# Block products for the first feed-forward's down projection, with a new order of the first batch's attention

## The chip, the cores and the metric

One core of a Trainium2 chip runs the kernel. The metric is the device time of one execution in microseconds (us), the median of several. TensorE (PE) multiplies into PSUM, a memory of eight banks; VectorE (DVE), ScalarE (ACT) and GpSimd (POOL) work on tiles in SBUF; SyncE (SP) issues nearly all transfers. A tile of 128x512 fp32 fills one PSUM bank.

## The reference

```python
kv  = einsum('bhsd,bhse->bhde', k, v)          # 4 batches, 8 heads, 576 rows, 64 wide
out = einsum('bhsd,bhde->bhse', q, kv)
x   = out / sqrt(mean(out*out, -1) + 1e-6) * g_norm      # 2304 tokens x 512
x   = (silu(x @ w_gate) * (x @ w_val)) @ w_out           # hidden 1536, weights in float64
y   = softplus(x @ w2_in) @ w2_out                       # hidden 2048, weights in float64
```

## The kernel before

Tokens lie in five tiles: one of 512 columns for each of the four batches (t = 0 to 3), and one of 256 columns for the 64 rows left over in each batch (t = B). Each fp32 product is made of three matmuls: every operand is split into a high part, rounded to fp32r, and a low part, the rest; `mm3` multiplies high by high, low by high and high by low and adds them in one PSUM bank. The high part is a cast on ScalarE, the low part a subtraction on VectorE or GpSimd. Weights come as 64-bit floats and are turned into fp32 by bit operations (`convert`: one ScalarE and three VectorE instructions).

**Attention.** For each batch `kv_step` (four), `q_step` (transposes, four or five), `o_step` and `x_step` run on TensorE. Between `o_step` and `x_step` stands the root: a square on ScalarE, sums and a small scaling on VectorE (L467, L468), a power of -0.5 on GpSimd (L469), and the multiplication with the result on VectorE (L473). Batch 0 is written out by a list of times (`S0`, `NORM0`, `SW`, `Q0`, `S1`); the later batches are woven into the first two hidden blocks of the first feed-forward.

**First feed-forward.** Hidden units go in 12 blocks of 128 (j). For each block and token tile, `ffn1_h` makes gate and value (24 matmuls into one bank each), `silu`, their product u, and u's high and low part (L565, L566). `ffn1_o` multiplies u with four column blocks of `w_out` (12 matmuls, each three into a bank of the pool `po` with three buffers), and VectorE adds each bank to the accumulator `yacc` (L583). The loop goes over j and, in it, over t; the down products of a tile run a tile or two behind its up products (`unit1`, `behind`).

**Second feed-forward.** It goes through pairs of hidden blocks (jp = 0 to 7), first for tokens of t = 0 and 1 (n = 0), then of t = 2 and 3 (n = 1). Its up products are block products already: seven instead of eight (`quad`, tiles hX, hY, hZ). Its down products for n = 1 are seven block products for jp below `LAST2` = 7 (`down2`, tiles dX, dY, dZ, 84 matmuls of 256 columns) and plain ones otherwise (`ffn2_o`, tile pz, 48 matmuls of 512 columns for two tiles). Sums of weight rows that `down2` needs are made beside n = 0 (`row_sums`, tiles pt), written to DRAM and read back.

**Order.** The program's order on every engine is fixed while it is built. A clock of the builder, `now`, runs on with each matmul (`tick`); work of the other engines is put in a queue with a time (`defer`), moved by hand-set shifts by name (`SHIFT`), and written out when the clock passes it. `ENGINE` says for single low parts whether VectorE or GpSimd makes them. On the chip each engine takes its instructions in that order and waits by semaphores.

## Time and profile before

| what | value |
|---|---|
| time, median of 3 runs | 895.47 us (894.54 to 895.49) |
| time of the profiled execution | 895.39 us |
| its span, first to last instruction | 893.3 us |
| TensorE busy | 872.4 us, 98% of the span |
| VectorE, ScalarE, GpSimd busy | 628.5, 352.9, 278.9 us |
| mean granted clock | 0.997 |

The span is 2.1 us shorter than the execution's time. A matmul's end in the profile is modelled, so the pace of matmuls is read from the starts of the next ones, not from their durations.

### The profile page before, as it was taken

The page shows a single profiled execution, that of the slowest core. Times are in us where ns is not written, and L with a number is a line of the kernel's source. Part 1 is how long each engine was busy: PE and PEld are TensorE (multiplying, and loading weights), DVE is VectorE, ACT ScalarE, POOL GpSimd, SP SyncE. Part 2 cuts the span into 40 slices and gives each one's busy share as a digit, 9 for nine tenths or more (in the row PEclk, how much of TensorE's full clock was granted, in tenths as well). Part 3 has the DMA queues.
Part 4 walks back from the last instruction along what each step waited for, and adds up shares of the span by engine and source line. Part 5 has one row for each costly group of instructions (what it writes and reads, how often), then busy time and mean ns, then how long its engine had stood idle before and what let it go on. Part 6 is the DMA issues. An engine that isn't in the chain of part 4 may idle for free.

```text
span 893.3 us, 12775 instructions
## 1 busy us (share of the span) xinstructions
PE 872.4 (98%) x4770; PEld 741.4 (83%) x4770; DVE 628.5 (70%) x987; ACT 352.9 (40%) x614; POOL 278.9 (31%) x211
## 2 busy tenths in 40 slices
PE   5899999999999999999999999999999999999998
PEld 4677788888888888888888888888887889999996
DVE  1865457877878687878687776776887667667564
ACT  3654435333332323233233454444564443444330
POOL 0642302303131312131222373355442132433321
PEclk9999999999999999999999999999999999999999
DMA  9963202234161526160515326667779865444213
GB/s 273 277 178 76 94 1 72 84 129 148 64 195 41 162 86 194 33 209 12 200 41 176 137 95 236 212 237 265 248 247 333 298 209 169 158 141 152 90 48 119
DMA packets 90766, 137.16 MB, mean 154 GB/s; under 512 B 20688, under 2 KB 51664, under 8 KB 90448
## 3 DMA queue, kind: packets, MB, share of 16 engines
q1 hardware_dynamic: 90400, 136.21, 46.4%
q8 instruction: 38, 0.62, 0.3%
q14 instruction: 24, 0.20, 0.1%
q10 hardware_dynamic: 304, 0.13, 0.1%
HBM read 99.09 MB, written 37.22 MB: 153 GB/s over the span
## 4 chain that ended last, share of the span: by engine, by line
PE 89%; DVE 4%; DMA 2%; SPq 2%; ACT 1%; issue 1%; POOL 0%; ACTq 0%; DVEq 0%; POOLq 0%
PE pv L523 16%; PE py L523 16%; PE pg L523 16%; PE pz L523 11%; PE hY L523 8%; PE dY L523 5%; PE hZ L523 4%; PE hr L523 3%; PE dZ L523 2%; PE hX L523 2%; PE pa L453 2%; DMA qr<-in_q_dram 1%; PE dX L523 1%; SPq L276 1%; DMA pt<-pt 1%
## 5 line engine op out<-in xcount | busy, mean ns | idle before, releaser
L583 DVE TENSOR_TENSOR yacc<-yacc,py 128x512 f32<-128x512 f32 (+1 forms) x220 | 136.5, 629 | 50.0 <-PE py L523 49.4
L565 ACT CAST uh<-u 128x512 fp32r<-128x512 f32 (+1 forms) x60 | 34.6, 577 | 168.1 <-DVE u L562 168.1
L523 PE MATMUL hY<-b,wh 128*128 128x512 f32 x384 | 98.2, 391 | 1.6 <-DVE c L908 1.6
L523 PE MATMUL pg<-xh,gh 128*128 128x512 f32 (+1 forms) x240 | 90.0, 375 | 0.0
L523 PE MATMUL pv<-xh,vh 128*128 128x512 f32 (+1 forms) x240 | 89.9, 375 | 0.0
L523 PE MATMUL py<-uh,oh 128*128 128x512 f32 (+1 forms) x240 | 89.5, 373 | 0.2 <-DVE yacc L583 0.2
L523 PE MATMUL py<-uh,ol 128*128 128x512 f32 (+1 forms) x240 | 88.6, 369 | 0.0
L523 PE MATMUL pg<-xl,gh 128*128 128x512 f32 (+1 forms) x240 | 88.5, 369 | 0.1
L523 PE MATMUL pv<-xh,vl 128*128 128x512 f32 (+1 forms) x240 | 88.6, 369 | 0.0
L523 PE MATMUL pg<-xh,gl 128*128 128x512 f32 (+1 forms) x240 | 88.4, 368 | 0.0
L523 PE MATMUL pv<-xl,vh 128*128 128x512 f32 (+1 forms) x240 | 88.4, 368 | 0.0
L523 PE MATMUL py<-ul,oh 128*128 128x512 f32 (+1 forms) x240 | 88.3, 368 | 0.0
L523 PEld LDWEIGHTS hY<-b,wh 128*128 128x128 f32 x384 | 70.2, 188 | 15.3 <-DVE c L908 2.0
L1055 DVE TENSOR_TENSOR zacc<-zacc,pz 128x512 f32<-128x512 f32 x77 | 52.3, 682 | 29.6 <-PE pz L523 29.5
L566 DVE TENSOR_TENSOR ul<-u,uh 128x512 fp32r<-128x512 f32 (+1 forms) x60 | 40.1, 669 | 39.1 <-ACT uh L565 39.1
L872 POOL TENSOR_TENSOR gl<-c,gh 128x512 fp32r<-128x512 f32 x33 | 44.4, 1350 | 53.6 <-ACT gh L870 45.7
L558 ACT ACTIVATE s<-pg 128x512 f32<-128x512 f32 (+1 forms) x60 | 33.2, 554 | 54.4 <-PE pg L523 49.2
L370 POOL TENSOR_TENSOR gl<-gz,gh 128x512 fp32r<-128x512 f32 x12 | 16.3, 1358 | 118.8 <-ACT gh L367 118.8
L523 PEld LDWEIGHTS pg<-xl,gh 128*128 128x128 f32 x240 | 45.2, 188 | 8.2 <-DVE xl L491 0.5
L523 PEld LDWEIGHTS py<-uh,oh 128*128 128x128 f32 x240 | 45.2, 188 | 8.0 <-DVE yacc L583 0.6
L523 PE MATMUL pz<-ph,gl 128*128 128x512 f32 x132 | 51.5, 390 | 0.4 <-POOL gl L872 0.4
L523 PEld LDWEIGHTS py<-ul,oh 128*128 128x128 f32 x240 | 45.1, 188 | 7.8
(198 smaller groups left out, 2059.3 us busy)
## 6 DMA issues: line engine op xcount, KB each, us to landing
wh<-w2d SPq DMA_DIRECT2D x32, 512.0 KB, 6.6
wh<-w2d SPq DMA_DIRECT2D x64, 256.0 KB, 4.7
ir<-in_moe_w_in_dram SPq DMA_DIRECT2D x16, 512.0 KB, 5.8
w2d<-kh SPq DMA_DIRECT2D x32, 256.0 KB, 2.1
w2d<-kl SPq DMA_DIRECT2D x32, 256.0 KB, 2.4
pr<-in_moe_w_out_dram SPq DMA_DIRECT2D x16, 512.0 KB, 6.6
pt<-pt SPq DMA_DIRECT2D x28, 256.0 KB, 6.8
tt<-pt SPq DMA_DIRECT2D x14, 512.0 KB, 6.9
```

The costliest lines, as they stand in the source:

```text
L276: nc.sync.dma_start(t.rearrange("p h c d -> p h (c d)"), src[b, h0:h0 + 4, 0:T, :].rearrange("h (p c) d -> p h (c d)", p=P))
L370: (nc.gpsimd if WLO1 == "g" else nc.vector).tensor_sub(lf, z, f32(hf))
L453: nc.tensor.matmul(pv[p0:p0 + n, hp, :], lhsT=qt[:, hp, p0:p0 + n], rhs=kvm[bb][:, hp, :], start=True, stop=True,)
L523: nc.tensor.matmul(dst, lhsT=a, rhs=b_, start=first and i == 0, stop=last and i == n - 1, skip_group_check=not check)
L558: nc.scalar.activation(s[0], pg, AF.Silu)
L565: nc.scalar.copy(uh, u)
L566: (nc.gpsimd if UL1 == "g" else nc.vector).tensor_sub(ul, u, f32(uh))
L583: defer(ADD1, lambda: nc.vector.tensor_add(a[:, d, :], a[:, d, :], p))
L872: (nc.vector if 0 <= n < len(GLO) and GLO[n] == "v" else nc.gpsimd).tensor_sub(lo, l, f32(hi))
L1055: defer(ADD2, lambda: nc.vector.tensor_add(av[:, m, :], av[:, m, :], p))
```

## The change

The down products of the first feed-forward go by pairs of hidden blocks (2jp, 2jp+1). For two token tiles, four blocks of u and four of `w_out` are multiplied as seven block products instead of eight: `release` makes four differences of u's blocks in place and seven high and low parts; `prep_o` makes four sums of `w_out`'s blocks, and four high and low parts where there were two; `down1` runs the seven products, each two steps of three matmuls, on two banks in turn, and adds the bank after every product to the accumulator before the next product adds to the same bank. Pair 0 (j = 0, 1) and the last pair (j = 10, 11) stay plain, and so does t = B; plain products now add both hidden blocks in PSUM before one addition to `yacc`. The up products are made pair by pair, with `prep_gv` loading and converting their weights. `LAST2` goes from 7 to 6, so that one more pair of n = 1 in the second feed-forward is multiplied plainly. In batch 0 the root is a `Sqrt` on ScalarE and a reciprocal on VectorE, with a table set loaded for it at the start and the one for `silu` after the batch's last `x_step`. `occupy` issues 29 matmuls of the identity with itself, whose result nobody reads, at five places of batch 0. The sums pt of `row_sums` lie in a buffer of their own, and the low part of the second feed-forward's `w_in` is made in place. The pool `pages` goes from 12 to 10 buffers. All times, `SHIFT` and `ENGINE` are new.

```diff
--- before.py
+++ after.py
...
-Q0 = [[9.4, 9.8, 10.2, 10.6], [26.45, 24.86, 29.33, 28.42]]
-S0 = [6.5, 8.0, 12.9, 14.05, 10.7, 11.1, 11.5, 11.51, 15.83, 15.8, 15.78, 17.6, 23, 27.55, 25, 27.19]
-S1 = [20.7, 21.9, 28.19, 27.76, 28]
-NORM0 = [1.34, 4.9, 5.92, 4.24]
-SW = [[13.46, 14.26, 15.06, 16.32, 18.51], [16.87, 17.67, 18.47, 19.27, 20.07]]
-
-
-
-NORM_AT = 3.28
+Q0 = [[10.03, 9.86, 10.2, 11.32], [21.59, 22.1, 21.97, 21.62]]
+S0 = [6.5, 8.0, 11.505, 11.506, 10.7, 11.1, 11.5, 11.57, 15.8, 15.86, 15.82, 15.83, 21.93, 20.1, 20.99, 20.3]
+S1 = [20.38, 20.22, 20.15, 21.13]
+NORM0 = [0.59, 1.0, 1.2, 1.3]
+SUM0 = [0.82, 0.7, -0.31, 0.97]
+SW = [[11.503, 11.504, 11.5041, 15.85, 15.86], [14.5, 14.14, 14.65, 18.1, 22.07]]
+
+
+
+NORM_AT = 3.19
...
+OCCUPY = {"k00": 10, "r00": 5, "q00": 7, "x00": 5, "x01": 2}
...
+SPLIT1 = ['11', '11', '11', '11', '00']
+COMB = [0.02, 1.8, 3.86]
+LEAD = 3
...
+P2_AT = [16.15, 40.02, 82.0, 106.0, 149.95, 174.0, 217.94, 241.01]
+PAGES = 10
...
-    wp = ctx.enter_context(tc.tile_pool(name="wp", bufs=2))
+    wp = ctx.enter_context(tc.tile_pool(name="wp", bufs=1))
...
-    pages = ctx.enter_context(tc.tile_pool(name="pages", bufs=12))
+    pages = ctx.enter_context(tc.tile_pool(name="pages", bufs=PAGES))
...
+    def occupy(at):
+
+        if at in OCCUPY:
+            if not spare:
+                spare.append(po.tile([P, P], F32, tag="po", name="spare"))
+            for _ in range(OCCUPY[at]):
+                nc.tensor.matmul(spare[0], lhsT=ident, rhs=ident, start=True, stop=True)
 
     def kv_step(b, hp):
+        occupy(f"k{b}{hp}")
...
-            nc.vector.tensor_copy(t[64:128, :, 64:128], pk[64:128])
+            (nc.scalar.copy if b == 0 else nc.vector.tensor_copy)(t[64:128, :, 64:128], pk[64:128])
...
-            nc.gpsimd.tensor_tensor(rs, ss, mhalf, op=ALU.pow)
+            if b == 0:
+                nc.scalar.activation(rs, ss, AF.Sqrt)
+            else:
+                nc.gpsimd.tensor_tensor(rs, ss, mhalf, op=ALU.pow)
 
         def norm():
+            if b == 0:
+                nc.vector.reciprocal(rs, rs)
...
+        if ch == (0, NC - 1):
+            nc.scalar.preload_act_table_set("silu_and_others")
...
+    def h1(j, t):
...
+            ru[j, t] = u
+            if t == B:
+                split_u((j, t), u, f"ub{j}")()
...
+    def split_u(name, src, key, default="v"):
+
+        w = src.shape[-1]
+        hl = []
+
+        def high():
+            if w == T:
+                hl.extend(up.tile([P, w], F32R, tag=t, name=f"{t}{key}") for t in ("uh", "ul"))
+            else:
+                hl.extend(up.tile([P, w], F32R, tag="u" + t, bufs=2, name=f"{t}{key}") for t in ("uh", "ul"))
+            nc.scalar.copy(hl[0], src)
+
+        def low():
+            (nc.gpsimd if en(f"{key}.e", default) == "g" else nc.vector).tensor_sub(hl[1], src, f32(hl[0]))
+            uc[name] = tuple(hl)
+
+        high = Step(high, *([order[0]] if order[0] and w == T else []))
+        if w == T:
+            order[0] = high
+        return Step(low, high)
...
+        b11, b12, b21, b22 = (ru.pop(x) for x in ((k0, t0), (k0, t1), (k1, t0), (k1, t1)))
+        lows = []
+
+        todo = []
+
+        def block(i, src, diff, *deps):
+            low = split_u((key, i), src, f"{key}_{i}", "g" if i % 2 else "v")
+            low.deps[0].deps += (diff,) * bool(diff) + deps
+            todo.append((diff, low.deps[0], low))
+            return low
+
+        l0 = block(0, b11, None)
+        l1 = block(1, b21, None)
+        d2 = minus(b11, b12, b11, l0)
+        l2 = block(2, b11, d2)
+        block(3, b22, None)
+        d4 = minus(b11, b22, b11, l2)
+        block(4, b11, d4)
+        d5 = minus(b12, b22, b12, d2)
+        block(5, b12, d5)
+        d6 = minus(b21, b21, b11, l1, d4)
+        block(6, b21, d6)
...
+    def down1(jp, n):
...
+        if n == NT // 2 or SPLIT1[jp - 1][n] == "0":
+            def plain(t, d):
+                p = po.tile([P, widths[t]], F32, tag="po", name=f"py{jp}_{t}_{d}")
+                mm3(p, [(tuple(x[:, d * P:(d + 1) * P] for x in need(ow, (jp, 3 * k_))), need(uc, (j, t)))
+                        for k_, j in enumerate((k0, k1))])
+                plus(acc_tile("y", t), d, p)
+                if jp == F1 // 2 - 1 and d == KD - 1:
+                    done_y(t)
+            return [lambda t=t, d=d: plain(t, d) for t in ([B] if n == NT // 2 else [2 * n, 2 * n + 1]) for d in range(KD)]
+
+        t0, t1 = 2 * n, 2 * n + 1
+        st = {}
+        KH = KD // 2
+
+        def mm(bank, d, first, i, a, half):
+            if first:
+                pool, tag = (ps, "ps") if bank == "Y" else (po, "po")
+                st[bank, d] = pool.tile([P, T], F32, tag=tag, name=f"p{bank}{jp}_{n}_{d}")
+            elif (bank, d, "w") in st:
+                st[bank, d, "w"]()
+            c = (half * KH + d) * P
+            mm3(st[bank, d], [(tuple(x[:, c:c + P] for x in need(ow, (jp, a))), need(uc, (key, i)))], first, True, check=False)
+
+        def out(bank, d, t, half):
+            f = plus(acc_tile("y", t), half * KH + d, st[bank, d])
+            st[bank, d, "w"] = f
+
+        def step(bank, d, first, i, a, half, t, o):
+            mm(bank, d, first, i, a, half)
+            out(bank, d, t, o)
+            if d == KH - 1:
+                more[key](i)
+            if jp == F1 // 2 - 1 and i == 6 and d == 1:
+                done_y(t0), done_y(t1)
+
+        steps = [("Y", True, 0, 0, 0, t0, 0), ("X", True, 1, 3, 0, t0, 0), ("Z", True, 2, 1, 0, t1, 1),
+                 ("Z", False, 3, 2, 1, t1, 0), ("Y", False, 4, 1, 1, t1, 0), ("Y", False, 5, 2, 0, t1, 1),
+                 ("Y", False, 6, 3, 1, t0, 1)]
+        return [lambda d=d, x=x: step(x[0], d, *x[1:]) for x in steps for d in range(KH)]
...
+    def prep_o(jp, at):
...
+            for i in range(4 if sums else 2):
+                k = (0, 3, 1, 2)[i]
+                z[k] = pages.tile([P, DM], F32, tag="pg", name=f"zo{jp}_{k}")
+            z["c"] = convert("o", 2 * jp, z[0]) + convert("o", 2 * jp + 1, z[3])
+            h = DM // 2
+            if sums:
+                z["m"] = mixes(z[0][:, :h], z[3][:, :h], z[0][:, h:], z[3][:, h:], z[1], z[2],
+                               [en(f"o{jp}.m{i}", "v") for i in range(4)])
...
-    LAST2 = F2 // 2 - 1
+    LAST2 = F2 // 2 - 2
...
-        nc.scalar.preload_act_table_set("silu_and_others")
+        nc.scalar.preload_act_table_set("sqrt_and_others")
...
-            f()
+            pair2(jp, P2_AT[jp])
+        behind = sum(behind, [])
+        prep_gv(3, A_AT)
+        prep_o(1, OW_AT)
+        for jp in range(1, F1 // 2):
+            k0, k1 = 2 * jp, 2 * jp + 1
+            end = jp == F1 // 2 - 1
+            if jp > 1:
+                prep_gv(k1, A_AT)
+                prep_o(jp, OW_AT)
+            weave(h1(k0, 0) + h1(k0, 1) + h1(k1, 0), (Q1_AT, behind))
+            weave(h1(k1, 1))
+            release(jp, 0)
+            weave(h1(k0, B) + h1(k1, B))
+            side0 = down1(jp, NT // 2) + down1(jp, 0)
+            if not end:
+                prep_gv(k0 + 2, B_AT)
+                weave(h1(k1, 2) + h1(k1, 3) + h1(k0, 2), (Q0_AT, side0))
+                weave(h1(k0, 3))
+                release(jp, 1)
+                behind = down1(jp, 1)
+            else:
+                defer(5.0, lambda: load_rows2(0))
+                rows2(0, 10.0)
+                weave(h1(k1, 2) + h1(k0, 2), (Q0_AT, side0))
+                side1 = down1(jp, 1)
+                release_plain(jp, 2)
+                blocks1(1)
+                load2(0)
+                h = h1(k1, 3) + h1(k0, 3)
+                weave(h[:6])
+                blocks1(B)
+                blocks1(2)
+                weave(h[6:], (O2_AT, side1[:KD]))
+                release_plain(jp, 3)
+                blocks1(3)
+                nc.scalar.preload_act_table_set("softplus")
+                weave(rest(0), (R0_AT, side1[KD:]))
...
```

## Rows read from the trace of the kernel before

**Rows 1.** The page: busy time by engine, share, instructions.
```profile
PE 872.4 (98%) x4770; PEld 741.4 (83%) x4770; DVE 628.5 (70%) x987; ACT 352.9 (40%) x614; POOL 278.9 (31%) x211
```

**Rows 2.** Waits of TensorE: for whom, total us, times, longest us.
```profile
PE kvp L404 <- DMA v<-in_v_dram: 7.0, 2, 6.7
...
PE px L484 <- DVE x L473: 2.3, 2, 1.8
...
PE hY L523 <- DVE c L908: 1.6, 1, 1.6
...
PE pq L436 <- ACT q L303: 1.5, 1, 1.5
...
PE kvp L414 <- DMA kvr<-in_v_dram: 1.1, 1, 1.1
...
PE py L523 <- DVE yacc L583: 0.2, 1, 0.2
```

**Rows 3.** Busy time of the engines in two stretches, one of each feed-forward.
```profile
151.78:188.82 37.04, 37.04 (x181) 31.32 (x181) 27.73 (x47) 11.83 (x21) 9.04 (x7) 1.00 0.37 129
...
750.19:775.55 25.36, 25.36 (x163) 23.08 (x163) 17.41 (x25) 9.88 (x18) 8.46 (x8) 1.00 0.50 167
```

**Rows 4.** Chain that ended last: start us, us, matmuls of 256 or 512 columns.
```profile
175.02 1.43 PE pg L523 x12
...
180.66 2.72 PE pg L523 x12
```

**Rows 5.** Timeline of TensorE, down products of 256 columns: start us, us.
```profile
868.75 0.28 PE L523 MATMUL dZ<-poh,gring 128*128 128x256 f32 x1
...
868.87 0.28 PE L523 MATMUL dZ<-pol,gring 128*128 128x256 f32 x1
```

**Rows 6.** Groups by line and form, 100 to 520 us: busy us, mean ns.
```profile
L583 DVE TENSOR_TENSOR yacc<-yacc,py 128x512 f32<-128x512 f32 x169 | 113.9, 683 | 41.2 <-PE py L523 40.7
...
L566 DVE TENSOR_TENSOR ul<-u,uh 128x512 fp32r<-128x512 f32 x44 | 32.1, 729 | 30.7 <-ACT uh L565 30.7
...
L352 DVE SCALAR_TENSOR_TENSOR zi<-ir,zi 128x512 int32<-128x512 int32 x16 | 15.0, 935 | 0.5
...
L653 POOL TENSOR_TENSOR kl<-zi,kh 128x512 fp32r<-128x512 f32 x16 | 21.2, 1325 | 45.5 <-ACT kh L648 21.9 <-PE py L523 10.4 <-DVE ul L566 6.8
...
L565 ACT CAST uh<-u 128x512 fp32r<-128x512 f32 x44 | 27.3, 620 | 123.2 <-DVE u L562 123.2
```

**Rows 7.** Timeline, TensorE and others at the start: start us, us, count.
```profile
12.36 3.65 PE L436 MATMUL pq<-ident,q 128*128 128x128 f32 x16 [1.52 <-ACT q L303]
...
15.94 1.12 PE L404 MATMUL kvp<-v,k 128*64 128x64 f32 x16
...
24.69 0.69 PE L404 MATMUL kvp<-v,k 128*64 128x64 f32 x16
...
28.07 2.94 PE L484 MATMUL px<-ident,x 128*128 128x128 f32 x12 [1.85 <-DVE x L473]
...
33.55 0.48 PE L523 MATMUL pg<-xh,gh 128*128 128x512 f32 x1
...
93.94 1.16 PE L453 MATMUL pa<-kv,qt 128*128 128x128 f32 x8
...
94.85 0.48 PE L523 MATMUL py<-uh,oh 128*128 128x512 f32 x1
...
22.54 6.58 POOL L469 TENSOR_TENSOR rs<-ss,mhalf 128x8 f32<-128x8 f32 x4 [20.76 <-DVE ss L468]
...
0.73 1.28 ACT L1152 ACT_TABLE_LOAD   x1 [0.73 <-PEq L1328]
...
30.70 0.62 ACT L303 COPY q<-qr 128x512 f32<-128x512 f32 x1 [1.21 <-DMA qr<-in_q_dram]
```

**Rows 8.** Busy time and granted clock (after POOL's), two early stretches.
```profile
24.00:26.00 2.00, 2.00 (x44) 1.72 (x41) 1.90 (x6) 0.89 (x2) 2.00 (x3) 1.00 1.09 349
...
30.00:32.00 2.00, 2.00 (x21) 1.55 (x21) 1.79 (x2) 1.29 (x3) 2.00 (x3) 0.51 1.09 332
```

More of the change, by code (lines that the diff above doesn't have):

```diff
@@ L412, in kv_step @@
         j = 64 * (b % 2)
+        occupy(f"r{b}{hp}")
         for e in range(2):
@@ L675, in load2 @@
             else:
-                hl = [wp.tile([P, DM], F32R, tag="ab"[i - 2] + "hl"[k_], name=f"wh{jp}_{i}{k_}") for k_ in range(2)]
+                hl = [wp.tile([P, DM], F32R, tag="ab"[i - 2] + "hl"[k_] + str(jp % 2), name=f"wh{jp}_{i}{k_}") for k_ in range(2)]
                 for k_ in range(2):
@@ L1026, in step @@
                 if k_ == 0:
-                    st["g"] = g_tiles() if jp == 0 else [pages.tile([P, T], F32R, tag="pg", name=f"g{x}r{jp}") for x in "hl"]
+                    st["g"] = g_tiles() if jp == 0 else None
+            if c == KD - 1 and st["g"] is None:
+                st["g", k_] = [up.tile([P, w], F32R, tag="uu" + x, bufs=2, name=f"g{x}r{jp}_{k_}") for x in "hl"]
             wh, wl = w2["h", jp, 3 * k_]
@@ L1298, in tile_linear_attention_two_ffn @@
                 seq = []
-                for f in main:
-                    seq += [f] + late[:1]
-                    late = late[1:]
+                for i, f in enumerate(main):
+                    k_ = 2 if n == 1 and jp and not i else 1
+                    seq += [f] + late[:k_]
+                    late = late[k_:]
                 for f in seq + late:
```

289 lines of the change are left out of this document (211 added, 78 removed), and 222 rows, old and new, of tables (ENGINE, SHIFT).

## The prediction

> **What bounds the kernel now.** I read the page first. TensorE is busy for 872.4 of 893.3 us, so 20.9 us are idle, and nothing beside TensorE comes near its share [rows 1]. A busy share can hide slow work, so the next view is who waited for whom on TensorE. The list is short: 7.0 us for the first values of batch 0, then 2.3, 1.5 and 1.1 us in the same batch's transposes and products, and one wait of 1.6 us late in the run. In the whole first feed-forward its down products waited once for VectorE's addition, for 0.2 us [rows 2].
>
> The windows say the same of one hidden block: TensorE fills 37.04 of 37.04 us, VectorE 27.73, ScalarE 11.83, GpSimd 9.04 [rows 3]. The pace comes from the chain: twelve matmuls of 512 columns take 2.72 us, 0.2267 each, and twelve of 256 columns 1.43 us, 0.119 each [rows 4]. A block has 144 of the former and 36 of the latter: 32.6 + 4.3 = 36.9 us, against 37.04 measured. So each matmul that goes away there gives back its 0.2267 us, as long as the other engines keep up.
>
> **Term 1: seven products for eight.** For two tiles and two hidden blocks the plain form has 2 x 2 x 4 x 3 = 48 matmuls of 512 columns. The new one has 7 products x 2 steps x 3 = 42. Six fewer, at 0.2267 us, are 1.36 us. `SPLIT1` takes it for four pairs and both halves, eight times: 48 matmuls, **-10.9 us**. The pair before needs 2 x 37.04 = 74.1 us, the pair after 71.4 us. Tile B and the last pair keep their matmuls.
>
> **Term 2: one pair fewer in the second feed-forward.** With `LAST2` at 6, pair 6 of n = 1 has 48 matmuls of 512 columns, 10.88 us, where it had 84 of 256. These start 0.12 us apart [rows 5], 10.1 us. By the other way, a period of 25.36 us [rows 3] less 54 matmuls of 512 columns and 24 of 256 leaves 10.3 us. So **+0.7 us** (0.6 to 0.8). Its row sums, casts and six transfers fall away; they lie beside a full TensorE and give nothing.
>
> **What the block products cost elsewhere.** Per pair VectorE loses four additions of 0.683 us (28 for 32), and gets eight differences of u's blocks and up to four half-wide sums of `w_out`. I price both by the subtraction of two SBUF tiles, 0.729 us [rows 6]: 5.8 and at most 2.9 us. Low parts go from 8 to 14; the default gives six to GpSimd, at 1.325 us, and `ENGINE` moves some either way, so I leave VectorE's eight as they are. VectorE: 55.5 - 2.7 + 5.8 + 2.9 = 61.5 of 71.4 us, 86%. GpSimd: 18.1 + 8.0 + 2.7 for two more low parts of `w_out` = 28.8 us, 40%. ScalarE gets eight casts of 0.620 us, 5 us, on 23.7. All three have room, so I cost these at nothing. The cover is TensorE's 71.4 us; VectorE's reserve is 9.9 us a pair, and each us beyond it is one on the path.
>
> Two new waits matter more than sums. First, a block's difference overwrites the tile that the block before was split from. One link is difference, cast, low part: 0.73 + 0.62 + 0.73 to 1.33 = 2.1 to 2.7 us. A product comes up about every 3.1 us (six of its matmuls and some eight of the woven up products, 14 x 0.2267), and `LEAD` = 3 products start ahead. Behind a late difference VectorE's own queue stands, the additions among it. Second, a product that adds to a bank waits until VectorE has added what the bank held. Three times in seven the same bank pair comes at once again. Between stand the other bank's step and about two and a half up steps, each 0.68 us: some 2.4 us, of which the addition needs 0.683. Before, three banks were in turn and the wait was 0.2 us in all; `down2` adds to standing banks in the same way, and its period holds TensorE at 25.36 of 25.36 us [rows 3]. So again nothing, at most 48 waits (3 x 2 x 8).
>
> **Term 3: the start.** The first up product starts at 33.55 us [rows 7]; what comes earlier moves all that follows. Three things stand before it. (a) Pace: sixteen kv matmuls take 1.12 us at 15.94 and 0.69 us at 24.69. So the early stretch runs at 0.62 of the later pace: 16 transposes of 3.65 us and two kv steps of 1.12 us could give 1.4 + 0.9 = 2.3 us. (b) The clock falls again: granted 0.51 at 30 to 32 us after 1.00 at 24 to 26 [rows 8], which are the levels 1.2 and 2.4 GHz; ahead of it TensorE waited 1.85 us for the root. Twelve transposes in 2.94 us and two more kv steps would give 1.1 + 0.9 = 2.0 us. (c) TensorE's wait of 2.3 us on the normalised x: GpSimd makes four powers one after another in 6.58 us, 1.65 each. A square root and a reciprocal of the same 128x8 tile have no row; a copy of 128x512 on ScalarE is 0.62 and a 128x512 operation on VectorE 0.73, so below 1.35 together and above nothing. All three: 6.6 us.
>
> Against it stand the unread products. One is two instructions; eight from 93.94 to 94.85 us make 0.23 us each at the higher pace, 0.37 at the lower. Ten lie in the 7.0 us wait, five meet one of 1.1, seven one of 1.5, seven one of 1.85. The overhang is 0.2 us at the higher pace and 2.6 at the lower; I take the middle, 1.3. VectorE may also take the value weights' bit operations ahead of the sums: two at 0.729 us [rows 6], 1.5. 6.6 - 1.3 - 1.5 = **-3.8 us**, bounds 0 and -6.6. The lower bound is 0 because batch 1's q lands only at 30.70 us, and the one tile that is ready before it has 24 up products for a block, 5.4 us.
>
> A second table load joins ScalarE's queue behind the last x, before the q copy of 30.70 us. The row of the load at the start is 1.28 us, which ends ahead of that copy if x is 2 us earlier, and 24 up products cover it otherwise. The Trainium skill's "ScalarE: Activation LUTs" (What ACT_TABLE_LOAD costs) puts a switch at 2.66 us with a drain that the row does not show; by it the copy would wait some 1 us and the sum would still be the same.
>
> **The rest.** The 1.6 us wait of hY hangs on row sums held up by their write to DRAM; these now have a buffer of their own and a wait on the former's write. I leave it: 0, bounds -1.6 and +1.6. The new times, ten instead of twelve buffers, and `w_in`'s low parts in place move work that lies beside a full TensorE: 0, with the rivals' prices.
>
> **The sum.** Against the profiled execution, 895.39 us with its span of 893.3 us: 895.4 - 10.9 + 0.7 - 3.8 = 881.4, say **881 us** (span 879). The median, 895.47, is 0.1 us off, which I neglect. 0.2%, 1.8 us, is about what a measurement of this kernel can tell from no change.
>
> **The rivals.**
>
> *The start does not move* (0.14). For it: everything up to 30 us is loaded at 332 to 349 GB/s [rows 8], and if second-half values or weights land late, a quicker root waits for them. Against: TensorE waited for transfers only for the first step. 895.4 - 10.2 = 885 us.
>
> *The start gives all and the late wait goes* (0.07). 895.4 - 10.2 - 6.6 - 1.6 = 877 us.
>
> *TensorE waits on its banks* (0.11). If the 48 additions come 0.2 us late each, 9.6 us are given back: 891 us. For it: VectorE goes from 75% to 86%. Against: the same scheme in the second feed-forward.
>
> *VectorE becomes the bound* (0.07), the one that ends slower. A bit operation on two SBUF tiles takes 0.935 us in L352, a subtraction of two 0.729 in L566: some 0.21 us lost on average [rows 6], at GpSimd's 24% of a block. About 20 of a pair's VectorE operations are of such a kind. At 0.21 us they add 4.2, inside the reserve of 9.9. If twelve wait for a whole GpSimd subtraction, 1.325 us, that is 15.9, 6.0 beyond, 24 us in four pairs: 905 us. It decides against the change from 13 us a pair on, ten such waits. The Trainium skill's "SBUF — State Buffer" (Who interferes with whom) says that a VectorE instruction with two SBUF inputs and a GpSimd instruction that reads SBUF lock each other out for their whole length. By that rule, and GpSimd at 40%, a mean wait would be 0.4 x 0.66 = 0.27 us, an estimate, and would stay hidden; the 0.21 us of L352 agrees.
>
> *Gain and new waits cancel* (0.04): a shortage in `pages`, which I can't place, at 1.8 us for each of eight halves gives 895 us.
>
> **The chances.** The forecast has 0.57, with a range of its own of 878 to 885. Faster by over 0.2%: forecast, start unmoved, start in full, nearly all of the banks' case, 0.88. Within 0.2%: 0.05. Slower: 0.07. The range of 876 to 888 holds the first three cases and the smaller half of the banks' case; left out are its larger half and the two last, under 0.2.
>
> **What the profile will show.** Right: a pair of blocks from equal place to equal place takes 71.4 us; the first `pg` starts near 29.5 us; no granted clock near 0.5 between 24 and 33 us; VectorE at 80 to 90% in the first feed-forward; TensorE's waits there under 1 us in all. Pair 6 of n = 1 lasts 26.1 us. Wrong: waits of py on `yacc` beyond 5 us in all (banks), VectorE above 95% there with subtractions above 1.0 us (bound), or a first `pg` later than 32 us (start).

## The result, and the profile after

The changed kernel takes 887.65 us (median of 4 runs, 887.20 to 888.28) against 895.0 us for the one before, a ratio of 0.9918 with a 95% interval of 0.9901 to 0.9936: 7.35 us faster. Forecast were 881 us and a range of 876 to 888. The profiled execution took 888.28 us, the slowest of the four, with a span of 886.5 us. Spans are compared below: 893.3 to 886.5, 6.8 us.

The page, busy time by engine, answers to [rows 1]:

```profile
PE 870.6 (98%) x4744; PEld 735.5 (83%) x4744; DVE 625.0 (71%) x981; ACT 366.4 (41%) x647; POOL 295.0 (33%) x225
```

TensorE's waits, total us, times and longest us, answer to [rows 2]:

```profile
PE px L649 <- DVE x L636: 2.4, 4, 1.4
PE pq L593 <- ACT q L444: 2.2, 3, 1.2
...
PE kvp L568 <- DMA kvr<-in_v_dram: 1.1, 1, 1.1
PE pz L690 <- POOL gl L1287: 1.1, 2, 0.7
...
PE pZ L690 <- DVE yacc L844: 0.7, 1, 0.7
PE hr L690 <- DMA wh<-w2d: 0.7, 2, 0.5
...
PE pY L690 <- DVE yacc L844: 0.3, 1, 0.3
```

The 7.0 us wait for the first values is in good part filled with unread products, and the 1.6 us wait of `hY` is gone. The 2.3 us wait for x is still there (2.4), and the first feed-forward now has waits of its own: `pZ` and `pY` for VectorE's additions, `hr` for weights.

Four pairs of the first feed-forward, from B's first gate product to the next; columns: stretch, length, busy PE, PEld, DVE, ACT, POOL, granted clock, share and rate of DMA. They answer to [rows 3]:

```profile
168.47:241.04 72.57, 71.85 (x351) 60.30 (x350) 59.94 (x103) 29.05 (x53) 27.44 (x22) 1.00 0.40 131
241.04:313.17 72.13, 72.05 (x350) 60.29 (x350) 64.53 (x106) 27.75 (x51) 26.04 (x19) 1.00 0.38 124
313.17:385.18 72.01, 71.69 (x350) 60.26 (x350) 61.84 (x96) 28.21 (x52) 39.00 (x29) 1.00 0.42 139
385.18:456.89 71.71, 71.59 (x350) 60.34 (x350) 57.31 (x98) 26.20 (x48) 23.61 (x18) 1.00 0.35 118
```

Forecast were 71.4 us a pair, VectorE at 86% and GpSimd at 40%. The pairs take 71.7 to 72.6, VectorE is busy for 80 to 89%, GpSimd for 33 to 54%. The pair that waits least, the last, is 0.3 us from the forecast.

**Where 6.8 us come from.** Three cuts serve: the last 16 products `pa` of batch 3 (107.26 us before, 106.12 after), the first `hY` of the second feed-forward (521.50 and 513.53) and the end.

| stretch | before | after | change | forecast |
|---|---|---|---|---|
| start to the last `pa` | 107.26 | 106.12 | -1.1 | -3.8 |
| on to the first `hY` | 414.24 | 407.41 | -6.8 | -10.9 |
| on to the end | 371.80 | 372.97 | +1.2 | +0.7 |

In the middle stretch the 48 matmuls are gone; 4.1 us came back as waits. Where the distance from one matmul's start to the next is more than 0.05 us above its usual 0.2267 us (512 columns) or 0.1195 us (256), the excess is called a gap here; the gaps of this stretch add up to 5.1 us after and 0.9 before. Of the 5.1 us, 2.4 are starts of `pZ` and `pY`, and 1.7 lie at `hr` and `py` between 504 and 509 us.

**The start.** Timelines after. ScalarE's part of the conversion of the first value weights:

```profile
19.69 0.67 ACT L490 ACTIVATE vz<-vr 128x512 f32<-128x512 f32 x1 [0.33 <-DMA vr<-in_moe_w_val_dram]
```

VectorE's first bit operation on them, its first row sum, the last normalised x:

```profile
20.39 0.43 DVE L493 TENSOR_SCALAR vz<-vz 128x512 int32<-128x512 int32 x1 [0.80 <-ACT vz L490]
...
22.19 0.68 DVE L625 TENSOR_REDUCE ss<-sq 128x8 f32<-128x512 f32 x1
...
29.12 0.69 DVE L636 TENSOR_TENSOR x<-pa,rs 128x512 f32<-128x512 f32 x1
```

Sum and x of the kernel before (L467 and L473), and some of what stands between them in VectorE's queue:

```profile
21.56 0.69 DVE L467 TENSOR_REDUCE ss<-sq 128x8 f32<-128x512 f32 x1
...
24.88 0.42 DVE L351 TENSOR_SCALAR vz<-vz 128x512 int32<-128x512 int32 x1
...
27.33 1.28 DVE L473 TENSOR_TENSOR x<-pa,rs 128x512 f32<-128x512 f32 x2
29.15 0.69 DVE L473 TENSOR_TENSOR x<-pa,rs 128x512 f32<-128x512 f32 x1 [0.53 <-POOL rs L469]
```

The last x starts at 29.15 us before and at 29.12 after: all that was done to TensorE's pace and to the root ahead of it moved it by nothing. In both kernels VectorE runs there almost without a stop, and in the one before it waited for GpSimd's power only 0.53 us. Ahead of the first sum the changed kernel waits for a transfer: ScalarE takes the value weights when they land, and VectorE's sums stand behind its bit operations on them. The first `pg` comes at 32.12 instead of 33.55 us because the way from the last x to it is shorter.

### The profile page after: what moved, and what is told of

It is laid out like the page before. It is cut to its first block, busy times and chain, and to the rows that moved or that the text cites. A ratio compares the mean times of both kernels' runs of the same rounds, so it can differ in the third digit from the quotient of the medians.

```text
span 886.5 us, 12733 instructions
## 1 busy us (share of the span) xinstructions
PE 870.6 (98%) x4744; PEld 735.5 (83%) x4744; DVE 625.0 (71%) x981; ACT 366.4 (41%) x647; POOL 295.0 (33%) x225
## 4 chain that ended last, share of the span: by engine, by line
PE 81%; DVE 10%; issue 2%; DMA 2%; ACT 2%; POOL 1%; SPq 1%; DVEq 0%; POOLq 0%; ACTq 0%
PE pz L690 14%; PE pv L690 13%; PE pg L690 13%; PE hY L690 9%; PE py L690 6%; PE hZ L690 5%; PE dY L690 4%; PE pY L690 4%; PE hX L690 2%; DVE yacc L844 2%; PE hr L690 2%; PE dZ L690 2%; PE pa L611 1%; PE pZ L690 1%; DMA vr<-in_moe_w_val_dram 1%
## 5 line engine op out<-in xcount | busy, mean ns | idle before, releaser
L1472 DVE TENSOR_TENSOR zacc<-zacc,pz 128x512 f32<-128x512 f32 x85 | 57.5, 683 | 44.9 <-PE pz L690 44.8
L774 POOL TENSOR_TENSOR ulc<-u,uhc 128x512 fp32r<-128x512 f32 x36 | 51.1, 1424 | 92.6 <-ACT uhc L771 61.4
L747 ACT ACTIVATE s<-pg 128x512 f32<-128x512 f32 (+1 forms) x50 | 27.7, 554 | 85.0 <-PE pg L690 82.8
L771 ACT CAST uhc<-u 128x512 fp32r<-128x512 f32 x64 | 38.9, 617 | 56.7 <-DVE u L783 48.0
L690 PEld LDWEIGHTS pv<-xl,vh 128*128 128x128 f32 x240 | 45.2, 189 | 7.6
L690 PE MATMUL pz<-pl,gh 128*128 128x512 f32 x132 | 51.4, 389 | 0.0
L690 PE MATMUL pz<-ph,gh 128*128 128x512 f32 x132 | 51.4, 389 | 0.0
L690 PEld LDWEIGHTS pg<-xh,gh 128*128 128x128 f32 x240 | 45.3, 189 | 7.1 <-ACT xh L655 0.2
L690 PEld LDWEIGHTS pv<-xh,vh 128*128 128x128 f32 x240 | 45.3, 189 | 6.9 <-issue 0.2
L690 PEld LDWEIGHTS pv<-xh,vl 128*128 128x128 f32 x240 | 45.3, 189 | 6.6
L690 PEld LDWEIGHTS pg<-xh,gl 128*128 128x128 f32 x240 | 45.3, 189 | 6.6
```

What stands on the lines that cost most here:

```text
L690: nc.tensor.matmul(dst, lhsT=a, rhs=b_, start=first and i == 0, stop=last and i == n - 1, skip_group_check=not check)
L747: nc.scalar.activation(s[0], pg, AF.Silu)
L771: nc.scalar.copy(hl[0], src)
L774: (nc.gpsimd if en(f"{key}.e", default) == "g" else nc.vector).tensor_sub(hl[1], src, f32(hl[0]))
L1472: defer(ADD2, lambda: nc.vector.tensor_add(av[:, m, :], av[:, m, :], p))
```

## The experiments

All were timed beside the kernel before, which took 894.8 to 895.3 us there (medians); the changed kernel's 887.65 us is the mark. For the start one table holds the kernels whose start differs: the time, in us, of the first products of k's and v's remainder rows (which wait for their transfer, unless marked *), and at which start VectorE's first row sum, the last x, the first `pg`, and the last `px` of batch 1; the last column is the distance from the first to the last.

| kernel | kvr | first sum | last x | first pg | last px | kvr to px |
|---|---|---|---|---|---|---|
| before | 8.90 | 21.56 | 29.15 | 33.55 | 53.89 | 45.0 |
| after | 9.80 | 22.19 | 29.12 | 32.12 | 52.62 | 42.8 |
| e2 | 9.29 | 25.26 | 32.20 | 35.20 | 55.69 | 46.4 |
| e3 | 8.96 | 21.00 | 31.82 | 34.03 | 54.02 | 45.1 |
| e6 | 10.29* | 21.23 | 28.17 | 31.23 | 51.72 | |
| e7 | 8.95 | 20.78 | 27.72 | 30.72 | 53.76 | 44.8 |
| e8 | 9.19 | 20.49 | 27.45 | 30.45 | 55.98 | 46.8 |
| e9 | 10.39* | 22.58 | 29.55 | 32.65 | 54.63 | |
| e11 | 9.78 | 21.06 | 28.02 | 31.13 | 53.10 | 43.3 |
| e12 | 9.18 | 20.46 | 27.43 | 30.43 | 53.34 | 44.2 |

**e1: the new order, no block products.**

```diff
-SPLIT1 = ['11', '11', '11', '11', '00']
+SPLIT1 = ['00', '00', '00', '00', '00']
```

> All five pairs of the first feed-forward multiplied plainly (SPLIT1 all 00), the rest as changed. My theory: the block products give 10.9 us of matmuls and lose about 2.6 us in waits of pZ and pY on VectorE's additions, so without them the time is 8.3 us longer, 896 us, and a pair of hidden blocks takes 74.1 us with no such wait. Rival: the changed order by pairs itself loses time in the first feed-forward; then waits of TensorE stay there and the time is 898 us or more. Second rival: the new order gives time of its own (half the additions), 893 us or less.

Measured: 903.43 us (902.82 to 903.88), ratio 1.009 (1.0075 to 1.0105) to the kernel before. Its span is 15.4 us above that of the changed kernel: 10.9 of matmuls and 4.5 of gaps more (9.5 for 5.1). Half of the gaps lie in one place; timeline of TensorE in e1:

```profile
221.47 0.80 PE L690 MATMUL py<-uhc,oh 128*128 128x512 f32 x1 [2.46 <-ACT uhc L771]
...
223.88 0.63 PE L690 MATMUL pg<-xh,gl 128*128 128x512 f32 x1
224.30 0.63 PE L690 MATMUL pg<-xl,gh 128*128 128x512 f32 x1
```

The wait is 2.46 us; then matmuls start 0.43 us apart up to 226, at a granted clock of 0.50, the lower level, so the wait is paid for about twice. The block products are worth their 10.9 us. My theory of 896 us fails, and the first rival holds on top: the order by pairs is no gain by itself, and in plain form, with times that were set for the block products, it loses.

**e2: no unread products.**

```diff
-OCCUPY = {"k00": 10, "r00": 5, "q00": 7, "x00": 5, "x01": 2}
+OCCUPY = {}
```

> The 29 unread products are left out. My theory: they hold TensorE's granted clock; without them the kv matmuls take 1.12 us for 16 again, the granted clock is near 0.5 in some stretch between 25 and 33 us, and the first pg starts 1 to 2 us later (33.1 to 34.1), 889 us. Rival: VectorE's queue sets when x is ready, whatever TensorE's pace; then the first pg stays within 0.5 us of 32.1 and the time within 0.5 us of 887.7.

Measured: 890.95 us (889.32 to 891.83), 3.3 us above the changed kernel. In the table the first sum comes 3.6 us later after `kvr`, and all behind it is equal to 0.01 us. The sixteen kv matmuls take 1.12 us again, as expected, but the granted clock reads 1.00 from 4 to 38 us, so the expected stretch near 0.5 did not come. The unread products bring what (a) and (b) of the forecast together less the overhang were priced at (3.0), and all of it ahead of the first sum.

**e3: the root back on GpSimd.**

```diff
-            if b == 0:
-                nc.scalar.activation(rs, ss, AF.Sqrt)
-            else:
-                nc.gpsimd.tensor_tensor(rs, ss, mhalf, op=ALU.pow)
+            nc.gpsimd.tensor_tensor(rs, ss, mhalf, op=ALU.pow)
...
-            if b == 0:
-                nc.vector.reciprocal(rs, rs)
...
-        if ch == (0, NC - 1):
-            nc.scalar.preload_act_table_set("silu_and_others")
```

The set for `silu` is loaded at the start here.

> Batch 0 takes its root by GpSimd's power again, with the table set for silu at the start and no second load. My theory: the root on ScalarE gave little, since the last square now waits on ScalarE behind a square root and VectorE works through the sums in the order written; the first pg starts between 32.0 and 33.2 us, the time is 887.5 to 888.7. Rival: the root is what the start gained; then the first pg starts at 33.5 us or later and the time is 889 us or more.

Measured: 889.4 us (889.25 to 892.87), 1.8 above the changed kernel, with the first `pg` at 34.03 us; my theory of a small effect falls, and the rival's two marks are met. From the first sum to the last x it is 10.82 us instead of 6.93. GpSimd in e3:

```profile
26.84 1.64 POOL L627 TENSOR_TENSOR rs<-ss,mhalf 128x8 f32<-128x8 f32 x1 [1.60 <-DVE ss L626]
30.15 1.64 POOL L627 TENSOR_TENSOR rs<-ss,mhalf 128x8 f32<-128x8 f32 x1 [1.68 <-DVE ss L626]
```

GpSimd waits for sums and VectorE for roots, in turn. The kernel before hid the powers behind the value weights' bit operations, which stood between sums and x there. The new order puts these ahead of the sums, and only then does the root on GpSimd cost 3.9 us. From the last x to the last `px` e3 is 1.3 us quicker, where no table load stands ahead of batch 1's q.

**e4: weights of the second feed-forward into the buffer that is free earlier.**

```diff
-                hl = [wp.tile([P, DM], F32R, tag="ab"[i - 2] + "hl"[k_] + str(jp % 2), name=f"wh{jp}_{i}{k_}") for k_ in range(2)]
+                hl = [wp.tile([P, DM], F32R, tag="ab"[i - 2] + "hl"[k_] + str((jp + 1) % 2), name=f"wh{jp}_{i}{k_}") for k_ in range(2)]
```

> The first weights of the second feed-forward go to the two buffers that hidden block 11 leaves instead of those of block 10, which is multiplied last. My theory: the transfers waited for the last reader of block 10's weights, so hr's waits on wh (0.26 and 0.45 us, with the pace lost around them 1.7 us) go and the time is 886.0 us. Rival: the transfers are late for SP's queue or the share of the DMA engines; then hr still waits and the time stays at 887.7.

Measured: 886.64 us (886.37 to 888.21). The waits of `hr` are gone; behind them a new one stands, in the same place:

```profile
505.79 0.50 PE L690 MATMUL py<-uhc,oh 128*128 128x512 f32 x1 [0.89 <-ACT uhc L771]
```

The gaps of this place are 1.7 us as before, so the late weights were not what bound it, and the theory fails. What stands behind them is VectorE's queue. In the changed kernel VectorE has there

```profile
502.56 2.99 DVE L1197 TENSOR_TENSOR b<-yacc,b 128x1024 fp32r<-128x1024 f32 x1
...
506.07 0.68 DVE L751 TENSOR_TENSOR u<-s,pv 128x512 f32<-128x512 f32 x1
```

and ScalarE

```profile
506.77 1.14 ACT L771 CAST uhc<-u 128x512 fp32r<-128x512 f32 x2 [3.48 <-DVE u L751]
```

The last pair's u is multiplied behind a low part of y that takes 2.99 us, and ScalarE's cast waits for u; in e4, which has the same order, `py` waits for that cast. Of the 1.6 us by which this profile's span is shorter, 1.0 came from the start, where nothing was changed (`kvr` at 9.32 instead of 9.80 us), and 0.7 from smaller gaps at other places. The times can't be told apart.

**e5: another order of the seven products.**

```diff
-        steps = [("Y", True, 0, 0, 0, t0, 0), ("X", True, 1, 3, 0, t0, 0), ("Z", True, 2, 1, 0, t1, 1),
-                 ("Z", False, 3, 2, 1, t1, 0), ("Y", False, 4, 1, 1, t1, 0), ("Y", False, 5, 2, 0, t1, 1),
+        steps = [("Y", True, 0, 0, 0, t0, 0), ("Z", True, 2, 1, 0, t1, 1), ("X", True, 1, 3, 0, t0, 0),
+                 ("Y", False, 4, 1, 1, t1, 0), ("Z", False, 3, 2, 1, t1, 0), ("Y", False, 5, 2, 0, t1, 1),
```

> One edit to the changed kernel (887.7 us): the seven block products of the first feed-forward run in the order 0, 2, 1, 4, 3, 5, 6, so that the two steps in bank Z and two of the three steps that meet in bank Y are parted by another bank's product. My theory: the 2.6 us that TensorE waits in the changed kernel for pZ and pY, 0.7 to 0.9 us at a time, come from a bank that is wanted again at once, while VectorE's addition stands behind differences and low parts; the waits of pZ and pY fall below 1 us and the time to 885.5 to 886. The rival: VectorE's queue is late whatever the order, so the waits move to other products (py on a low part, or pY at the place where two steps still meet): 887.7 us, unchanged.

Measured: 893.55 us (891.13 to 896.38, 10 runs), 5.9 above the changed kernel, worse than both theories. (The blocks of u are released in the new order too.) The waits for `pZ` go, but the gaps grow from 5.1 to 11.3 us. The largest, on TensorE, and what VectorE did meanwhile:

```profile
263.45 0.39 PE L690 MATMUL pY<-uhc,ol 128*128 128x512 f32 x1
266.26 0.50 PE L690 MATMUL pY<-ulc,oh 128*128 128x512 f32 x1 [2.42 <-DVE ulc L774]
...
268.18 0.63 PE L690 MATMUL pg<-xh,gh 128*128 128x512 f32 x1
```

```profile
263.73 0.42 DVE L493 TENSOR_SCALAR gz<-gz 128x512 int32<-128x512 int32 x1
264.18 0.69 DVE L494 SCALAR_TENSOR_TENSOR gz<-gr,gz 128x512 int32<-128x512 int32 x1
264.91 0.69 DVE L498 SCALAR_TENSOR_TENSOR gz<-gr,gz 128x512 int32<-128x512 int32 x1
265.52 0.68 DVE L774 TENSOR_TENSOR ulc<-u,uhc 128x512 fp32r<-128x512 f32 x1
```

A low part that TensorE wants at once stands behind three bit operations for weights that are wanted later; `pX` meets late additions as well (1.5 us). So the rival is right in kind: VectorE was late in this order too. The times were set by hand for the other one; what this order could do with times of its own wasn't tried.

**e6: the third q step behind the k steps, all o steps ahead of the first sums.** Two shifts: `'a0.6'` from -0.48 to 0.2, `'a0.11'` from 1.99 to 0.9.

> Two times of the builder in batch 0 of the changed kernel: the third q step stands behind the last two k steps, where it was ahead of them, and all o steps stand ahead of the first sums, so that ScalarE's last square does not stand behind a square root that waits for VectorE. My theory: the new order holds the start up by the 1.24 us that TensorE waits for a copy of q in front of the k steps and part of the 1.86 us that ScalarE's root waits for sums; the first gate product comes 1 to 2 us earlier, measured from the end of the wait for the first k and v, and the time is 886 to 886.7. The rival: the last x hangs on VectorE's queue, where the bit operations of the value weights stand ahead of the sums: no change, 887.7.

Measured: 887.33 us (886.70 to 887.72), not to be told from the changed kernel. The wait of 1.24 us for q is gone, and a wait of 0.67 us for v's transfer stands in its place; sum to x and x to `pg` are what they were (6.94, 3.06). The rival fits: the sums still stand behind the bit operations on the value weights.

**e7: the value weights' conversion behind the x.**

```diff
-SW = [[11.503, 11.504, 11.5041, 15.85, 15.86], [14.5, 14.14, 14.65, 18.1, 22.07]]
+SW = [[11.503, 11.504, 11.5041, 15.85, 15.86], [20.0, 20.0, 22.6, 28.6, 22.07]]
```

> Five times of the builder: the value weights of block 0 are turned into fp32 behind the first batch's normalisation and not ahead of its sums; VectorE has those operations behind the x multiplications. My theory: the sums start about 1.5 us earlier, the first x and with it the first gate product 1 to 1.8 us earlier, and the value product still finds its weights because 12 gate matmuls (2.7 us) lie ahead of it: 886 to 886.7. The rival: the value weights then come late and TensorE waits for them between gate and value, as long as was saved: 887.7; a third, that ScalarE's order and not VectorE's holds x up: 887.7 without that wait.

Measured: 891.12 us (889.09 to 891.52), 3.5 above the changed kernel. First half right: the first sum comes 0.6 us earlier after `kvr`, so do the last x and the first `pg`. Then 2.5 us are lost up to the last `px`, since ScalarE's part of the conversion stands ahead of what batch 1 needs. The profile is of the fastest of the four runs, 889.09 us; where the others lose another 2 us isn't shown.

**e8: e6 and e7 together.**

> The edits of e6 and of e7 together. My theory: each holds back the other's gain, since x needs the last square as well as the sums; together they bring the first gate product 2 to 3 us earlier, near the 29.5 us that was forecast, and the time to 885 to 886. The rival, that the start is bound by the landing of the loads and the pace of TensorE: no more than 0.5 us, 887.2.

Measured: 890.68 us (889.66 to 890.95). The first `pg` comes at 30.45 us, 1.7 earlier (1.1 earlier after `kvr`), and the last `px` 3.4 later. ScalarE, and then TensorE, in e8:

```profile
34.31 0.62 ACT L509 CAST vh<-vz 128x512 fp32r<-128x512 f32 x1 [1.44 <-DVE vz L498]
34.84 0.61 ACT L444 COPY q<-qr 128x512 f32<-128x512 f32 x1
```

```profile
36.32 2.05 PE L611 MATMUL pa<-kv,qt 128*128 128x128 f32 x8 [2.04 <-ACT qt L597]
```

The cast waits for VectorE, behind it stands the copy of batch 1's q, behind that the transposed q, and TensorE waits. The window of e8 behind the wait (columns as above):

```profile
38.00:42.00 4.00, 4.00 (x17) 3.67 (x17) 2.96 (x6) 2.27 (x4) 2.00 (x2) 0.50 0.71 192
```

The granted clock is 0.50 for these four microseconds, so that this wait too costs more than its length. The rival named a bound ahead of the first product, the landing of the loads, and that is met as well: with the third q step behind the k steps TensorE waits for the next v, here 1.26 us at 14.91.

**e9: VectorE's part behind the x, the cast behind the first copies of q.** The edits of e6, `SW[1]` as [14.5, 22.6, 22.65, 3.0, 4.3], the last two counted from the first feed-forward's start.

> The edits of e6, and in place of those of e7: ScalarE's part of the first value weights' conversion stays ahead of the x, VectorE's three bit operations come behind the last low part of x, and the cast and the low part of these weights come after the first q copies of batch 1. My theory: VectorE's queue is the bound of the start (from the first conversion to the last x it never stops in e6), and e7 gave its gain back since the cast stood in ScalarE's queue ahead of a copy of q that TensorE needs; here the first gate product starts 1.5 to 2 us earlier than in e6 and no wait over 1 us follows on TensorE before 45 us: 885 to 886. The rival: the copies of q follow the landing of batch 1's q and not the queue, so that TensorE waits for them whatever comes before: 887.3, as e6.

Measured: 887.76 us (887.55 to 889.65). The theory fails on both halves. The first `pg` comes at 32.65 us, 1.4 later than in e6: this profile is of the slowest of the four runs, v lands 0.7 us later in it than in e6, and the 32 products `pa` take 4.62 us instead of 3.81, at a granted clock of 0.50 from 18 to 20 us. In e11, which has the same start, the first `pg` comes 1.0 us earlier after `kvr` than in the changed kernel. And behind the first `pg` TensorE waits 0.42 us for kv, 0.55 for the transposed q and 0.70 for the value weights' low part, and the way from `pg` to the last `px` is 22.0 instead of 20.5 us.

**e10: two bit operations behind the additions of pZ.** One shift, `'o2.c1'` from -0.24 to 1.9. In the changed kernel VectorE's queue there is

```profile
222.78 0.69 DVE L774 TENSOR_TENSOR ulc<-u,uhc 128x512 fp32r<-128x512 f32 x1
223.38 0.69 DVE L783 TENSOR_TENSOR u<-u,u 128x512 f32<-128x512 f32 x1
223.98 0.42 DVE L493 TENSOR_SCALAR zo<-zo 128x512 int32<-128x512 int32 x1
224.44 0.69 DVE L494 SCALAR_TENSOR_TENSOR zo<-or,zo 128x512 int32<-128x512 int32 x1
225.05 1.28 DVE L844 TENSOR_TENSOR yacc<-yacc,pZ 128x512 f32<-128x512 f32 x2
```

and TensorE waits at 225.78 us for the first of these additions, though the last matmul into its bank had started at 221.95.

> One time of the builder in the changed kernel: two bit operations on w_out in pair 2 go behind the two additions of pZ that they stood ahead of. My theory: the wait of 0.72 us for pZ near 225 us (0.9 us with the slower start behind it) comes from these alone; it goes, nothing else moves, and the time is 886.7, a change below what the times tell but not below what the trace tells. The rival: the sums of w_out are late for the next product and TensorE waits there as long: 887.7.

Measured: 887.06 us (886.38 to 887.75). The wait for `pZ` is gone, so its cause is shown: the addition's place in VectorE's queue, not its length. But a later product waits now; timeline of TensorE in e10:

```profile
230.31 0.47 PE L690 MATMUL pY<-uhc,oh 128*128 128x512 f32 x1 [0.60 <-ACT uhc L771]
```

That is 0.8 us of gap for 1.0. The rival is right in the amount; what is late is not a sum of `w_out` but a cast of u, which waits for a difference in VectorE's queue (L783). In both kernels VectorE runs without a stop from 217 to 232 us, so that moving one piece of its work only moves the wait.

**e11: e4, e9 and e10, and block products for the last pair's first half.** `SPLIT1` ends in `'10'`.

> The edits of e4, e9 and e10 together, and the last pair's first half as block products too (eight matmuls-of-512 groups: 6 matmuls less, 1.36 us). My theory: start 2 us, the pZ wait 0.9, the wait for weights 0.7, the matmuls 1.36, and about 1 us of new waits at the last pair, which has little time for differences: 883 to 884. The rival: the last pair's block products end later than the plain ones, since their casts stand behind VectorE's 2.99 us low part of y, and eat the 1.36: 885.

Measured: 897.99 us (897.00 to 898.84), 10.3 above the changed kernel for 1.36 us of matmuls less. The gaps are 16.5 us. TensorE and VectorE in e11:

```profile
486.03 0.39 PE L690 MATMUL pv<-xl,vh 128*128 128x512 f32 x1
491.16 0.77 PE L690 MATMUL pY<-uhc,oh 128*128 128x512 f32 x1 [4.74 <-DVE yacc L844]
```

```profile
486.99 1.03 DVE L493 TENSOR_SCALAR pz<-pz 128x512 int32<-128x512 int32 x1 [3.25 <-ACT pz L490]
488.06 1.63 DVE L494 SCALAR_TENSOR_TENSOR pz<-pr,pz 128x512 int32<-128x512 int32 x1
...
490.33 1.28 DVE L844 TENSOR_TENSOR yacc<-yacc,pY 128x512 f32<-128x512 f32 x2
```

VectorE itself waits 3.25 us with a conversion at the head of its queue, and the additions that free TensorE's banks stand behind it. Two more waits for additions, 1.62 and 1.72 us, lie at 448 and 482 us. Theory and rival both fall: this is what the prediction's rival of the banks describes, in a place where block products had not stood, with times set for other work.

**e12: e4, e6, and the conversion in a third place.** ScalarE's part ahead of the squares, VectorE's behind the copies of q and kv: `SW[1]` as [10.4, 0.3, 0.35, 2.2, 2.5], the last four from the first feed-forward's start.

> The edits of e4 (weights of the second feed-forward into the other buffer) and e6, and the first value weights' conversion in a third place: ScalarE's part ahead of the squares, where VectorE never waits for it, VectorE's bit operations behind the copies of batch 1's q and kv, then the cast and the low part. My theory: the first gate product starts 1.2 us earlier after the first product of q and kv than in the changed kernel, the three waits that e9 had behind it (kv 0.4, qt 0.6, value weights' low part 0.7 us) go, 0.7 us of the wait for weights goes: 885.2 to 886. The rival: as in e7, e9 and e11, each us saved ahead of the first gate product is waited for behind it: 887.

Measured: 889.19 us (888.66 to 889.26). The first `pg` comes 1.1 us earlier after `kvr`, the way on to the last `px` is 2.4 us longer, with a wait of 1.49 us for the transposed q, again behind the cast of the value weights on ScalarE. The rival is right, and by more than it said.

## Why the prediction was right, and where it was not

The direction and the range held, and the forecast by itself was 6.7 us too low. That the range held is in part luck: 887.65 us lies 0.35 us inside its end and one of the four runs outside, and two of the steps below failed, both the same way. Of the prediction's signs VectorE's share and the clock came; a first `pg` near 29.5 us and waits under 1 us in the first feed-forward did not; the 26.1 us of pair 6 can't be read off, as its products stand among those of its neighbours. Against the profiled execution, 881.4 forecast and 888.28 measured, the terms are these.

**Term 1 held.** The pair periods and e1 show it: 48 matmuls, 10.9 us.

**Term 2** measured +1.2 for +0.7 us with all else in that stretch. The matmuls exchanged are 48 for 84, as forecast, +0.8 us at their paces. The wait of `hY` for c is gone (-1.6, inside its bounds), but other gaps more than took it back (4.9 us in all for 4.0), among them a new wait of 0.7 us for `gl` on GpSimd; the way from the last matmul to the end is 0.5 us shorter. Which edit made these gaps wasn't tested.

**What the block products and the new times cost elsewhere, put at nothing, was the larger of the two failed steps**: 4.1 us came back, 2.4 of them at the banks ("again nothing") and 1.7 in the step to the second feed-forward ("work that lies beside a full TensorE: 0"). The argument for the banks was that some 2.4 us lie between two products in one bank and the addition takes 0.683. The addition did take 0.68; it stood in a queue. VectorE took it behind a low part, a difference and two bit operations (e10), though its bank was full. The Trainium skill's "Perfetto Trace Analysis" (Tensor Engine Instruction) says of VectorE, ScalarE and GpSimd that they are "strict FIFO"; these rows agree. So not the reserve of 9.9 us a pair counts but the place of each piece, and e5 and e11 show what a wrong place costs. The reserve lies elsewhere in the pair: all waits for additions fall into stretches of 10 us and more in which VectorE was never idle for more than 0.06 us. The prediction did name VectorE's queue, with the additions behind a late difference, but priced it at zero.

*TensorE waits on its banks* therefore holds in part: 2.4 us, not 9.6. The other 1.7 us look in the list of waits like late weights; e4 took that wait away and the 1.7 us stayed, with the last pair's cast behind VectorE's low part of y in the place of the weights.

**VectorE as the bound** did not come for a pair as a whole. Groups of the changed kernel by line, 100 to 520 us, answer to [rows 6]:

```profile
L774 POOL TENSOR_TENSOR ulc<-u,uhc 128x512 fp32r<-128x512 f32 x36 | 51.1, 1424 | 92.6 <-ACT uhc L771 61.4 <-DVE yacc L844 12.4 <-issue 12.3
...
L783 DVE TENSOR_TENSOR u<-u,u 128x512 f32<-128x512 f32 x32 | 24.1, 753 | 1.4 <-POOL ulc L774 1.2
...
L774 DVE TENSOR_TENSOR ulc<-u,uhc 128x512 fp32r<-128x512 f32 x28 | 21.6, 774 | 0.5
```

Differences and low parts take 0.75 and 0.77 us for 0.73; beside the kernel before the loss on VectorE stays below 0.05 us each, on GpSimd it is 0.1. The 15 of these 60 VectorE operations that overlap a GpSimd subtraction take 0.96 us on average, the other 45 take 0.70.

**Term 3, the start, was the other failed step**: -3.8 forecast, -1.1 measured. The first k and v remainders were ready at 9.80 instead of 8.90 us. Their transfers are issued at the same times in both kernels (within 0.03 us), and in the other runs of this program that varies from 8.95 to 9.78; of the kernel before there is one trace, so how much of these 0.9 us is chance stays open. The mark that the prediction set for this case, a first `pg` later than 32 us, was met at 32.12. From `kvr` on the start is 2.2 us shorter. By its parts (first sum, last x, `pg`, last `px`, from the table) these are 12.66, 7.59, 4.40 and 20.34 us before, 12.39, 6.93, 3.00 and 20.50 after.

(a) was to give 2.3 us ahead of the first sum and gave 0.3. TensorE did run at the higher pace (e2: 3.6 us), but the new order took nearly all of it back: the third q step waits 1.24 us, and the value weights' bit operations, 1.8 us, stand ahead of the sums. That these come first was in the sum, at 1.5; what was missed is that in the kernel before they filled the time of the root, and that they wait for a transfer. In the changed kernel, e1, e5 and e10 ScalarE waits 0.24 to 0.37 us for the value weights to land, and the first sum comes 2.5 us after that, whatever the landing (19.3 to 19.7 us). Where the conversion was moved and the k steps come earlier (e8, e11, e12) TensorE waits 1.26 us for v, and the first sum comes 5.6 us after that:

```profile
14.88 0.69 PE L557 MATMUL kvp<-v,k 128*64 128x64 f32 x16 [1.26 <-DMA v<-in_v_dram]
```

(e12). So what the rival *the start does not move* was made of, values and weights that land late, holds for the way to the first sum. The prediction argued against it that TensorE had waited for transfers only for the first step; its own row had two waits for v, and a start that is moved ahead meets transfers that are not.

(c) was to give 2.3 us and gave 0.7. TensorE's wait, put down to the root, was read from its list of waits (2.3 us, the longest 1.85). VectorE's own rows say that the root held it up for 0.53; for the rest it was busy with sums, x and conversions. With the square root on ScalarE the stretch from the first sum to the last x is 6.93 to 6.97 us in eight kernels of the table, whatever was moved around it: four sums, four scalings, four reciprocals and four multiplications on VectorE, which by their rows add up to 7.0 of the 7.6 us to the end of the last x. There VectorE is the bound, and the prediction looked for its share in hidden blocks only. (Its list of TensorE's waits was short of two as well: 1.4 us for transposed q and 1.0 us for kv, both ahead of `pa`.)

(b) was to give 2.0 us. No granted clock near 0.5 stands between 24 and 33 us any more, as forecast, and the way from the last x to the first `pg` is 1.4 us shorter. But e2 has the same 3.00 us there and the same clock of 1.00 without one unread product, so they did not bring it. Behind the end of the last x the changed order has one kv step fewer, one step of transposes of x more, and its q step comes behind the first `pg` (`pq` at 34.05); kv step and q step took 0.87 and 0.42 us there before. How much the pace gives beside that wasn't separated. The forecast also counted two kv steps at the lower pace where the trace before has one: 1.12 us at 30.94, but 0.69 at 32.26.

Could the missing part be had? e7, e8, e9 and e12 moved the value weights' conversion and lost what they won again behind the first `pg`, on ScalarE and VectorE, where batch 1's q, kv and weights pass through the same two queues. That the start can be no shorter isn't shown; none of the five orders tried (e6 to e9, e12) was faster in all. No version here is faster than the changed kernel by more than the runs can tell (e4: 886.64 us).

The second table load cost what its row says and no more:

```profile
32.09 1.28 ACT L657 ACT_TABLE_LOAD   x1
33.38 1.14 ACT L444 COPY q<-qr 128x512 f32<-128x512 f32 x2
```

ScalarE's instruction before it ended at 32.08 us. The Trainium skill's "ScalarE: Activation LUTs" (What ACT_TABLE_LOAD costs) has 2.66 us for a switch, a drain included; these rows show the 1.28 us and no drain on either side, so here the load is taken at 1.28. It did delay the q copy: `pq` waits 0.57 us at 34.05.

## What to carry to other kernels

Before a wait of the main engine is priced, read the queue of the engine that it names: if that engine ran without a stop, the step it seems to wait for isn't the bound, and making that step faster gives only the idle time in that queue. A reserve of 10 or 20% on a helper engine does not hide work that is wanted at a certain moment; look at what stands ahead of it in program order, and whether the engine has any idle time in that stretch. When taking away what a wait names leaves the time as it was (e4, e10), look for what stands behind it. And when a start is made shorter, follow it to the next place where all engines must have caught up, since most of what is won ahead of the first product can be lost right behind it.

## What the runs showed of the hardware

A wait of TensorE of some two microseconds or more cost up to twice its length. After 2.46 us (e1), 2.42 (e5) and 4.74 (e11) matmuls of 512 columns started 0.43 us apart, at a granted clock of 0.50, the lower of the two levels, for 4.5, 3.0 and 5.3 us; in e5 the fall came 1.5 us behind the wait. Waits of 0.3 to 0.7 us (changed kernel, e10), and of 1.62 and 1.72 us in e11, cost 0.2 to 0.3 us more than their length, since the next starts came a little late.

The granted clock does not tell the pace by itself. The 32 products `pa` of batch 0 in e2 and, below, in the changed kernel:

```profile
20.84 5.82 PE L611 MATMUL pa<-kv,qt 128*128 128x128 f32 x32
```

```profile
18.84 3.81 PE L611 MATMUL pa<-kv,qt 128*128 128x128 f32 x32 [0.36 <-issue]
```

The granted clock is 1.00 in both from 18 to 28 us. The edit between the kernels is the 29 unread products alone, of which TensorE had done 22 by then.
